# Gate and value products of four chunks by Strassen's scheme, with partial sums added in DRAM, in an attention kernel with two feed-forward layers

## The chip, the core and the metric

The kernel runs on one core of a Trainium2 chip. The metric is the device time of one execution in microseconds, the median of several. The engines are named as in the profile: PE is TensorE's matmuls (PEld its weight loads), DVE VectorE, ACT ScalarE, POOL GpSimd, SP the engine that does nothing but start transfers. Each takes its instructions in the order of its own queue.

## The reference

All is computed in fp32; the inputs arrive as float64 in their bit patterns. Linear attention over 4 batches of 576 rows and 8 heads of 64 gives a matrix x of 2304 tokens by 512. Two feed-forward layers follow:

```python
gate = 1.0 / (1.0 + np.exp(-(x @ w_gate)))      # w_gate, w_val: 512 x 1536
x = (gate * (x @ w_val)) @ w_out                # w_out: 1536 x 512
h = x @ w_in                                    # 512 x 2048
out = np.maximum(0.01 * h, h) @ w_out2          # 2048 x 512
```

## The kernel before

Each fp32 matrix is held as a sum of two fp32r parts, hi and lo (`split`, line 47: a CAST on ACT gives hi, a subtraction on DVE gives lo). One product of such matrices is three matmuls (`mm3`, lines 51 to 54: hi by hi, hi by lo, lo by hi), so L52, L53 and L54 of the profile are those three. The tokens lie transposed in five blocks: blocks 0 to 3 are 512 tokens of a batch, block 4 (called B in the code) the 4 times 64 that are left, 256 wide. A pair is blocks 0 and 1, or 2 and 3.

A layer's hidden width is worked off in chunks of 256, six in the first layer and eight in the second. The weights of a chunk come as float64 words over SP's queue (`fetch`) and are decoded to hi and lo on DVE and ACT (`decode`, lines 91 to 109) by the generator `decoded`, which is driven a step at a time by `ahead` wherever the code has room for it, and fully by `need` where a weight is wanted.

The attention comes first, with the first chunk of layer 1 for blocks 0 to 2 woven in. Layer 1 then goes, chunk by chunk and block by block, through `up_plain`: per half chunk a gate and a value product of 4 times 3 matmuls each, Tanh on ACT, one instruction on DVE that forms (tanh + 1) times value, and `hidden`, which splits the result into gh and gl. `down1_piece` multiplies those by w_out (6 matmuls into a PSUM bank ps_p) and adds the bank to the sums `acc` in SBUF on DVE (line 639). Pieces wait in the list `pend` until `gap` takes them out between later products, so that PE has work while DVE and ACT make the next gh and gl.

Layer 2 handles a pair at a time by Strassen's scheme (`quad`, lines 728 to 787): seven block products in place of eight, with sums of weight quarters (`sh`, `sl`, made in `decoded` where `quarters` is true) and sums of activation blocks (`sum_steps`, `sum_parts`; planes T1 to T4 in `ts`). The results leave `quad` in the order 3, 0, 2, 1; result i belongs to half i // 2 of the chunk and block i % 2 of the pair. SBUF holds the planes of one pair alone. After its last use in the first pair of a chunk each plane is overwritten with the other pair's from DRAM, by `swap` on SP's queue (line 726, tile `w<-td`); the first time it is computed in place and stored (line 712). A chunk of layer 2 is the units pair, B, pair, and the next chunk goes the other way round, so it begins with the pair that the last one ended on. After block B's unit the pieces of the first pair are worked off, block 2u + 1 ahead of block 2u (line 859).

Instructions are put in an order per engine by a scheduler at build time; the order is fixed in the program.

## Time and profile before

| | |
|---|---|
| median of 3 runs | 1069.11 us (1065.23 to 1069.24) |
| the profiled execution | 1071.7 us, its span 1069.9 us |
| granted TensorE clock, mean | 0.998 |
| busy share of PE, DVE, ACT, POOL | 97%, 69%, 42%, 5% |
| share of PE in the chain that ended last | 74% (DVE 11%, DMA 9%) |
| moved by DMA | 104.46 MB, mean 98 GB/s |

The profile lists for each engine how long it was busy, what ended its idle time, and when each instruction began. Matmuls overlap: one is listed as busy for 0.39 us while the next begins 0.23 us after it, so times of PE are read from starts, not from busy times. Stages follow one another: attention to about 311 us, five chunks of layer 1 to about 683 us, then eight chunks of layer 2.

### The profile page before, as it was taken

What the parts mean: (1) busy time and instruction counts of PE and PEld (TensorE: products, weight loads), DVE (VectorE), ACT (ScalarE), POOL (GpSimd) and SP (SyncE); (2) the same over time, 40 slices, a digit from 0 to 9 for tenths busy, and PEclk for the clock granted to TensorE, in tenths of its full rate; (3) what the DMA queues carried; (4) which work ended last, traced back from release to release, by engine and by line L of the source; (5) the groups of instructions that cost most, each with busy time, mean ns of one, the idle gap of its engine ahead of it and who ended that gap; (6) DMA issues with size and microseconds to landing.
All of it is one profiled execution on the core that took longest, in us unless ns stands there. A gap on an engine that the chain in (4) does not pass through costs nothing.

```text
span 1069.9 us, 14566 instructions
## 1 busy us (share of the span) xinstructions
PE 1041.7 (97%) x5506; PEld 886.0 (83%) x5506; DVE 741.4 (69%) x1309; ACT 454.2 (42%) x954; POOL 50.9 (5%) x49
## 2 busy tenths in 40 slices
PE   7899999999999999999999999999999999999997
PEld 6788988889788888888888888888888788887886
DVE  4964777766379985393493439995688787978555
ACT  4666676766454332131131124574333243423221
POOL 0112121212200000000000000000000000000000
PEclk9999999999999999999999999999999999999999
DMA  6532242331263321030030003435153351615233
GB/s 148 147 82 69 68 114 63 78 81 49 83 216 118 118 79 40 1 104 16 1 118 1 1 0 157 176 101 197 60 176 116 121 178 59 216 40 177 69 139 128
DMA packets 96006, 104.46 MB, mean 98 GB/s; under 512 B 66112, under 2 KB 66240, under 8 KB 95936
## 3 DMA queue, kind: packets, MB, share of 16 engines
q1 hardware_dynamic: 95936, 103.52, 31.1%
q8 instruction: 44, 0.72, 0.3%
q14 instruction: 26, 0.21, 0.1%
HBM read 87.10 MB, written 16.33 MB: 97 GB/s over the span
## 4 chain that ended last, share of the span: by engine, by line
PE 74%; DVE 11%; DMA 9%; ACT 3%; SPq 2%; issue 1%; POOL 1%; POOLq 0%; DVEq 0%
PE ps_u L52 11%; PE ps_u L53 11%; PE ps_u L54 11%; PE ps_p L54 10%; PE ps_p L52 10%; PE ps_p L53 9%; PE kv L384 4%; DMA raw<-in_moe_w_out_dram 3%; PE ps_n L434 2%; DMA raw<-in_moe_w_in_dram 2%; DVE acc L808 2%; DMA raw<-in_moe_w_gate_dram 1%; DVE w L108 1%; DVE ql L419 1%; DVE m L101 1%
## 5 line engine op out<-in xcount | busy, mean ns | idle before, releaser
L52 PE MATMUL ps_u<-xh,w 128*128 128x512 f32 (+1 forms) x592 | 213.8, 361 | 0.6 <-ACT w L106 0.4
L53 PE MATMUL ps_u<-xl,w 128*128 128x512 f32 (+1 forms) x592 | 213.7, 361 | 0.2 <-DVE xl L49 0.2
L54 PE MATMUL ps_u<-xh,w 128*128 128x512 f32 (+1 forms) x592 | 213.2, 361 | 0.0
L52 PEld LDWEIGHTS ps_u<-xh,w 128*128 128x128 f32 x592 | 111.8, 189 | 18.3 <-ACT xh L48 0.6
L53 PEld LDWEIGHTS ps_u<-xl,w 128*128 128x128 f32 x592 | 111.8, 189 | 17.4 <-DVE xl L49 0.5
L54 PEld LDWEIGHTS ps_u<-xh,w 128*128 128x128 f32 x592 | 111.7, 189 | 17.2 <-DVE w L108 0.2
L52 PE MATMUL ps_p<-w,gh 128*128 128x512 f32 x288 | 113.4, 394 | 5.8 <-ACT gh L48 5.8
L808 DVE TENSOR_TENSOR acc<-acc,ps_p 128x512 f32<-128x512 f32 x126 | 85.8, 684 | 41.4 <-PE ps_p L54 41.3
L48 ACT CAST gh<-q 128x512 fp32r<-128x512 f32 (+1 forms) x134 | 76.6, 575 | 88.4 <-DVE q L663 86.7
L53 PE MATMUL ps_p<-w,gh 128*128 128x512 f32 x288 | 112.4, 390 | 0.0
L54 PE MATMUL ps_p<-w,gl 128*128 128x512 f32 x288 | 111.4, 392 | 0.9 <-DVE gl L49 0.4
L49 DVE TENSOR_TENSOR gl<-q,gh 128x512 fp32r<-128x512 f32 (+1 forms) x134 | 83.8, 632 | 31.4 <-ACT gh L48 30.9
L663 DVE SCALAR_TENSOR_TENSOR q<-q,ps_u 128x512 f32<-128x512 f32 (+1 forms) x54 | 33.7, 625 | 87.1 <-PE ps_u L54 79.0
L674 ACT ACTIVATE q<-q 128x512 f32<-128x512 f32 x48 | 30.1, 630 | 123.4 <-DVE q L751 123.4
L97 ACT ACTIVATE e<-e,ebias 128x512 int32<-128x512 int32 x68 | 49.1, 723 | 77.9 <-DVE e L96 77.6
L53 PE MATMUL ps_p<-gl,w 128*128 128x512 f32 (+1 forms) x216 | 79.1, 366 | 0.0
L54 PE MATMUL ps_p<-gh,w 128*128 128x512 f32 (+1 forms) x216 | 79.0, 366 | 0.0
L52 PE MATMUL ps_p<-gh,w 128*128 128x512 f32 (+1 forms) x216 | 78.8, 366 | 0.2 <-ACT gh L48 0.2
L639 DVE TENSOR_TENSOR acc<-acc,ps_p 128x512 f32<-128x512 f32 (+1 forms) x100 | 62.7, 632 | 22.6 <-PE ps_p L54 21.3
L52 PEld LDWEIGHTS ps_p<-w,gh 128*128 128x128 f32 x288 | 54.1, 188 | 19.1 <-ACT gh L48 8.6
L54 PEld LDWEIGHTS ps_p<-w,gl 128*128 128x128 f32 x288 | 54.1, 188 | 15.0 <-DVE gl L49 3.9
L751 DVE TENSOR_TENSOR q<-ps_u,q 128x512 f32<-128x512 f32 x80 | 54.9, 688 | 16.3 <-PE ps_u L54 12.4
(144 smaller groups left out, 2017.5 us busy)
## 6 DMA issues: line engine op xcount, KB each, us to landing
w<-td SPq DMA_DIRECT2D x56, 512.0 KB, 6.0
raw<-in_moe_w_out_dram SPq DMA_DIRECT2D x28, 512.0 KB, 3.5
raw<-in_moe_w_in_dram SPq DMA_DIRECT2D x16, 512.0 KB, 3.7
td<-w SPq DMA_DIRECT2D x16, 512.0 KB, 2.7
raw<-in_moe_w_gate_dram SPq DMA_DIRECT2D x12, 512.0 KB, 4.3
raw<-in_moe_w_val_dram SPq DMA_DIRECT2D x12, 512.0 KB, 3.9
rb<-rd SPq DMA_DIRECT2D x32, 144.0 KB, 3.2
k<-in_k_dram SPq DMA_DIRECT2D x32, 128.0 KB, 2.9
```

The lines of the kernel that those rows point to most:

```text
L48: nc.scalar.copy(hi, src)
L49: nc.vector.tensor_tensor(out=lo, in0=src, in1=hi.bitcast(F32), op=ALU.subtract)
L52: nc.tensor.matmul(ps, lh, rh, start=first, stop=False, **kw)
L53: nc.tensor.matmul(ps, lh, rl, start=False, stop=False, **kw)
L54: nc.tensor.matmul(ps, ll, rh, start=False, stop=last, **kw)
L97: nc.scalar.activation(out=e, in_=e, func=ACTF.Relu, scale=8.0, bias=ebias)
L384: nc.tensor.matmul(ps[:, h], p.kf[j // 2][:, j % 2, h, s, :], vf[:, j, 64 * h:64 * h + 65], start=(h, j) == (0, 0), stop=False)
L639: nc.vector.tensor_tensor(out=a, in0=a, in1=po, op=ALU.add)
L663: nc.vector.scalar_tensor_tensor(out=th, in0=th, scalar=1.0, in1=ps[1], op0=ALU.add, op1=ALU.mult)
L674: nc.scalar.activation(out=th, in_=t, func=ACTF.Lrelu)
L751: nc.vector.tensor_tensor(out=o, in0=x, in1=y, op=ALU.add)
L808: nc.vector.tensor_tensor(out=a, in0=a, in1=po, op=ALU.add)
```

## The change

Chunks 2 to 5 of layer 1 (four of six) use `quad` for gate and for value (`up_pair1`, new), which takes 7 products where `up_plain` took 8. For that the weights of these chunks get quarter sums (`halved`), and x gets planes T: `norm3` stores x to DRAM (`xd`), `first_sums` loads it back and builds the planes in chunk 1. The planes of the two pairs are exchanged once a chunk, in both layers, by transfers that GpSimd's queue starts (`load_sums`). Layer 1's sums no longer stay in SBUF: in chunks 1 to 4 ACT copies a finished bank into one of six staging halves and GpSimd's queue adds it to DRAM (`accum_op`), and chunk 5 loads the sums back (`load_acc`). Block 2u now comes ahead of 2u + 1 in the pieces of both layers. Some hunks are left out (signatures, names, the exact slots).

```diff
+    def halved(l, c, i):
+
+        return i < 2 and (l, c) >= (1, 2)
...
-            while len(free) < (4 if quarters else 2) + reserve[0]:
+            quarters = halved(*key)
+            while len(free) < (4 if quarters else 2) + reserve[0] or key[:2] >= hold[0]:
...
+        nc.sync.dma_start(out=xd[b][:, c], in_=p.rb[:, 0:MAIN])
...
+    def staging():
+        staged[0] += 1
+        return halves[staged[0] % 6]
...
+
+        for i in range(1 if b == B else 2):
             acc(1, b, 2 * i)
-            nc.sync.dma_start(out=sums[1, b, i][0].rearrange("p (k t) -> p k t", k=2), in_=accd[b][:, 2 * i:2 * i + 2])
+            a = sums[1, b, i][0]
+            if b == B:
+                nc.sync.dma_start(out=a.rearrange("p (k t) -> p k t", k=KD), in_=accd[b])
+            else:
+                nc.sync.dma_start(out=a.rearrange("p (k t) -> p k t", k=2), in_=accd[b][:, 2 * i:2 * i + 2])
...
+            ahead(1)
+            if c == 0:
+                first_sum(b, e, po, staging())
+                return
+            if c < NC1 - 1:
+                st = staging()[:, :bw[b]]
+                nc.scalar.copy(st, po)
+                nc.gpsimd.dma_start(out=accd[b][:, e], in_=st, accum_op=ALU.add)
+                return
             a = acc(1, b, e)
-            if c == 0:
-                nc.scalar.copy(a, po)
-                return
             nc.vector.tensor_tensor(out=a, in0=a, in1=po, op=ALU.add)
...
                 if f == 0:
-                    gap(100)
+                    gap(4)
...
-    def sum_parts(pair, n, place=None):
+    def sum_parts(l, pair, n, s):
 
         j, i = PLACE[n]
-        src = sums.pop((1, 2 * pair + i, j))
-        s = [take(F32R) for _ in range(2)] if place is None else [retake(p) for p in place]
+        src = sums.pop((l - 1, 2 * pair + i, j))
         hi, lo = s[0][0], s[1][0]
         nc.scalar.copy(hi, src[0])
         nc.vector.tensor_tensor(out=lo, in0=src[0], in1=hi.bitcast(F32), op=ALU.subtract)
         give(src)
-        ts[n] = s
-        td[pair, n] = dr.tile([128, 2, 1024], F32, name=f"td{pair}{n}", tag=f"td{pair}{n}")
+        td[l, pair, n] = dr.tile([128, 2, 1024], F32, name=f"td{l}{pair}{n}", tag=f"td{l}{pair}{n}")
         for k in range(2):
-            nc.sync.dma_start(out=td[pair, n][:, k], in_=s[k][0].bitcast(F32))
+            nc.sync.dma_start(out=td[l, pair, n][:, k], in_=s[k][0].bitcast(F32))
...
+    def first_sums(pair, stay):
+
+        for i in range(2):
+            for j in range(2):
+                s = sums[0, 2 * pair + i, j] = take(F32, "acc")
+                nc.sync.dma_start(out=s[0].rearrange("p (k t) -> p k t", k=2), in_=xd[2 * pair + i][:, 2 * j:2 * j + 2])
+        for _ in range(8):
+            yield True
+        yield from sum_steps(1, pair)
+        held = deque()
+        for n in (2, 1, 3, 4):
+            if len(held) == 2:
+                give(*held.popleft())
+            s = [take(F32R) for _ in range(2)]
+            sum_parts(1, pair, n, s)
+            if stay:
+                ts[n] = s
+            else:
+                held.append(s)
+            yield True
...
+    def load_sums(l, pair, n):
+        for k in range(2):
+            nc.gpsimd.dma_start(out=ts[n][k][0].bitcast(F32), in_=td[l, pair, n][:, k])
...
+    def swap(l, pair, n):
+
         ts[n] = [retake(s) for s in ts[n]]
-        for k in range(2):
-            nc.sync.dma_start(out=ts[n][k][0].bitcast(F32), in_=td[other, n][:, k])
-
-    def quad(l, c, i, pair, then):
+        if (l, pair, n) in td:
+            load_sums(l, pair, n)
+        else:
+            sum_parts(l, pair, n, ts[n])
+
+    def quad(l, c, i, pair, rooms, then):
...
+    def up_pair1(c, pair, between, then):
+        h, th = {}, {}
+        for i, t in quad(1, c, 0, pair, (1, 1, 1, 1, 1, 0), lambda n: None):
+            th[i] = halves[6 + i]
+            nc.scalar.activation(out=th[i], in_=t, func=ACTF.Tanh, scale=0.5)
+        between()
+        for i, t in quad(1, c, 1, pair, (1, 1, 1, 0, 0, 0), then):
+            nc.vector.scalar_tensor_tensor(out=th[i], in0=th[i], scalar=1.0, in1=t, op0=ALU.add, op1=ALU.mult)
+            hidden(h, (i // 2, 2 * pair + i % 2), th[i])
+        return h
...
+    def queue1(c, u, h):
+        bs = [B] if u == B else [2 * u, 2 * u + 1]
+        pend.extend(down1_piece(c, b, e, h) for b in bs for e in range(KD))
+
...
+        h = up_plain(1, 0, b, 14)
+        gap(100)
+        pend.extend(down1_piece(0, b, e, h) for e in range(KD))
...
+    side.append(first_sums(0, False))
+    for b in range(NB):
+        reserve[0] = (4, 8, 8, 5, 2)[b]
...
-                    sum_parts(0, n)
-            if b == B:
-                drop(1, c, 0)
+            side[:] = [first_sums(1, True)]
+        h = up_plain(1, 1, b, 5)
+        gap(100)
...
+    units = [1, B, 0]
+    keep = lambda n: None
+    for c in range(2, NC1):
+        final = c == NC1 - 1
+        if final:
+            units = [0, 1, B]
+        for n, u in enumerate(units):
+            if u == B:
+                h = up_plain(1, c, B, 2)
+            elif not final:
+                h = up_pair1(c, u, (lambda: drop(1, c, 0)) if n == 2 else (lambda: None),
+                             (lambda k, u=u: swap(1, 1 - u, k)) if n == 0 else keep)
+            elif u == 0:
+                def between():
+                    need(1, c, 1)
+                    need(1, c, 2)
+                    hold[0] = 2, 0
+
+                def then(k):
+                    swap(1, 1, k)
+                    if k == 4:
+                        gap(2)
+                        load_acc(0)
+                        load_acc(1)
+                h = up_pair1(c, 0, between, then)
+            else:
+                def between():
...
+                def then(k):
+                    for g in side:
+                        for _ in g:
+                            pass
+                    side.clear()
+                    swap(2, 0, k)
+                reserve[0] = 5
+                h = up_pair1(c, 1, between, then)
+                drop_sums(1, c, 1)
...
-            pend.extend(down1_piece(c, b, e, h) for e in range(KD))
-            if b == B:
...
+    need(2, 0, 0)
+    for _ in sum_steps(2, 1):
...
+                hold[0] = 3, 0
...
-            bs = [B] if u == B else [2 * u + 1, 2 * u]
+            bs = [B] if u == B else [2 * u, 2 * u + 1]
             pend.extend(down2_piece(c, b, j, h) for b in bs for j in range(bw[b] // 128))
```

The built program has, against the one before, on PE 96 fewer matmuls of 512 columns; on DVE 80 more additions of a PSUM bank (`q<-ps_u,q`), 64 fewer of 512 and 16 fewer of 256 columns into `acc`, 16 more 1024 wide (x's planes), 32 more of 256 and 16 more of 512 for weight sums; on ACT 88 copies of a bank to staging, 16 to q, and 16 CASTs 1024 wide more; on POOL 168 transfers where there were none (88 planes `w<-td`, 80 additions to `accd`); on SP 56 planes fewer, 16 plane stores, 16 stores and 8 loads of x more.

Three places show how the order moves. Line numbers of the two kernels differ: before, L663 is gate times value, L639 the addition into `acc`, L643 the lo part of layer 1's result, L695 and L707 sums and lo parts of planes, L751 an addition in `quad`, L174 a weight sum's lo part; after, these are L869, L681, L685, L738, L749, L822 and L180, while L105 to L114 decode a weight.

First, DVE in a chunk of layer 1, before:

```order
L663 SCALAR_TENSOR_TENSOR q_4827<-q_4827,ps_u_4829 128x512
L49 TENSOR_TENSOR gl_4844<-q_4827,gh_4843 128x512
L663 SCALAR_TENSOR_TENSOR q_4865<-q_4865,ps_u_4867 128x512
L639 TENSOR_TENSOR acc_3670<-acc_3670,ps_p_4885 128x512
L49 TENSOR_TENSOR gl_4882<-q_4865,gh_4881 128x512
L639 TENSOR_TENSOR acc_3670<-acc_3670,ps_p_4893 128x512
L639 TENSOR_TENSOR acc_3672<-acc_3672,ps_p_4901 128x512
L639 TENSOR_TENSOR acc_3672<-acc_3672,ps_p_4909 128x512
L663 SCALAR_TENSOR_TENSOR q_4941<-q_4941,ps_u_4943 128x512
L49 TENSOR_TENSOR gl_4958<-q_4941,gh_4957 128x512
```

and after, the end of a pair's value products:

```order
L869 SCALAR_TENSOR_TENSOR w_4590<-w_4590,q_5366 128x512
L869 SCALAR_TENSOR_TENSOR w_4589<-w_4589,ps_u_5306 128x512
L180 TENSOR_TENSOR w_5469<-s_5610,w_5468 128x512
L49 TENSOR_TENSOR gl_5390<-w_4590,gh_5389 128x512
L49 TENSOR_TENSOR gl_5395<-w_4589,gh_5394 128x512
L822 TENSOR_TENSOR q_5315<-ps_u_5307,q_5315 128x512
L822 TENSOR_TENSOR q_5323<-ps_u_5308,q_5323 128x512
L869 SCALAR_TENSOR_TENSOR w_4590<-w_4590,q_5315 128x512
L869 SCALAR_TENSOR_TENSOR w_4589<-w_4589,q_5323 128x512
L180 TENSOR_TENSOR w_5469<-s_5610,w_5468 128x512
L49 TENSOR_TENSOR gl_5411<-w_4590,gh_5410 128x512
L49 TENSOR_TENSOR gl_5423<-w_4589,gh_5422 128x512
```

The additions of ps_p into `acc` are gone from DVE there; additions inside `quad` (L822) and weight sums (L180) stand in their place.

Second, DVE where layer 2 begins. Before, from the last of the four sums of the second pair's blocks:

```order
L695 TENSOR_TENSOR acc_3672<-acc_3672,acc_3860 128x1024
L751 TENSOR_TENSOR q_6807<-ps_u_6791,q_6799 128x512
L707 TENSOR_TENSOR w_6810<-acc_3860,w_6809 128x1024
L639 TENSOR_TENSOR acc_3984<-acc_3984,ps_p_6816 128x256
L639 TENSOR_TENSOR acc_3984<-acc_3984,ps_p_6826 128x256
L174 TENSOR_TENSOR w_6924<-s_7060,w_6923 128x512
L707 TENSOR_TENSOR w_6843<-acc_3670,w_6842 128x1024
L643 TENSOR_TENSOR xl4_95<-acc_3984,xh4_94 128x256 x2
L639 TENSOR_TENSOR acc_3984<-acc_3984,ps_p_6849 128x256
L751 TENSOR_TENSOR q_6865<-ps_u_6791,q_6799 128x512
L643 TENSOR_TENSOR xl4_95<-acc_3984,xh4_94 128x256
L707 TENSOR_TENSOR w_6868<-acc_3843,w_6867 128x1024
```

and after, from the third of them (w_71xx and w_72xx are planes, m_7105 a weight of layer 2 being decoded, acc_6924 block B's sums, xh4 and xl4 its parts):

```order
L738 TENSOR_TENSOR acc_6922<-acc_6922,acc_6916 128x1024
L107 SCALAR_TENSOR_TENSOR m_7105<-raw_7082,m_7105 128x512
L738 TENSOR_TENSOR acc_6918<-acc_6918,acc_6922 128x1024
L749 TENSOR_TENSOR w_7133<-acc_6922,w_7132 128x1024
L681 TENSOR_TENSOR acc_6924<-acc_6924,ps_p_7141 128x256
L111 SCALAR_TENSOR_TENSOR m_7105<-m_7105,e_7106 128x512
L685 TENSOR_TENSOR xl4_95<-acc_6924,xh4_94 128x256
L681 TENSOR_TENSOR acc_6924<-acc_6924,ps_p_7152 128x256
L749 TENSOR_TENSOR w_7171<-acc_6916,w_7170 128x1024
L685 TENSOR_TENSOR xl4_95<-acc_6924,xh4_94 128x256
L114 TENSOR_TENSOR w_7104<-m_7105,w_7103 128x512
L105 TENSOR_SCALAR m_7105<-raw_7093 128x512
```

The decoding of a weight now stands between the planes and block B's parts.

Third, layer 2 after block B's unit. PE before, where gh_8154 is the last result of the pair and gh_8101 the first:

```order
L54 MATMUL ps_u_8193<-xh4_94,w_7778 128x256
L52 MATMUL ps_p_8213<-w_8009,gh_8154 128x512
L53 MATMUL ps_p_8213<-w_8010,gh_8154 128x512
L54 MATMUL ps_p_8213<-w_8009,gl_8155 128x512
L52 MATMUL ps_p_8213<-w_8009,gh_8101 128x512
L53 MATMUL ps_p_8213<-w_8010,gh_8101 128x512
L54 MATMUL ps_p_8213<-w_8009,gl_8102 128x512
```

and after, where gh_8050 is the second result and gh_8084 the third:

```order
L54 MATMUL ps_u_8127<-xh4_94,w_7712 128x256
L52 MATMUL ps_p_8147<-w_7943,gh_8050 128x512
L53 MATMUL ps_p_8147<-w_7944,gh_8050 128x512
L54 MATMUL ps_p_8147<-w_7943,gl_8051 128x512
L52 MATMUL ps_p_8147<-w_7943,gh_8084 128x512
L53 MATMUL ps_p_8147<-w_7944,gh_8084 128x512
L54 MATMUL ps_p_8147<-w_7943,gl_8085 128x512
```

ACT makes them, before:

```order
L674 ACTIVATE q_8105<-ps_u_7986 128x512
L48 CAST gh_8107<-q_8105 128x512
L674 ACTIVATE q_7995<-q_7995 128x512
L97 ACTIVATE e_8465<-e_8465,ebias_74 128x512
L48 CAST gh_8134<-q_7995 128x512
L97 ACTIVATE e_8598<-e_8598,ebias_74 128x512
L674 ACTIVATE q_8003<-q_8003 128x512
L171 CAST w_8187<-s_8312 128x1024
L48 CAST gh_8154<-q_8003 128x512
L674 ACTIVATE q_8179<-ps_u_8166 128x256
```

and after, with gh_8096 the last result:

```order
L716 ACTIVATE q_8048<-ps_u_7920 128x512
L48 CAST gh_8050<-q_8048 128x512
L103 ACTIVATE e_8399<-e_8399,ebias_74 128x512
L177 CAST w_8121<-s_8246 128x1024
L716 ACTIVATE q_7929<-q_7929 128x512
L48 CAST gh_8084<-q_7929 128x512
L716 ACTIVATE q_7937<-q_7937 128x512
L716 ACTIVATE q_8113<-ps_u_8100 128x256
L48 CAST gh_8096<-q_7937 128x512
```

PE's first piece after block B now reads the second and third result of the pair where it read the last.

## Rows read from the trace of the kernel before

**Rows 1.** The page's head and its part 1: span, busy time of each engine, instructions

```profile
span 1069.9 us, 14566 instructions
...
PE 1041.7 (97%) x5506; PEld 886.0 (83%) x5506; DVE 741.4 (69%) x1309; ACT 454.2 (42%) x954; POOL 50.9 (5%) x49
```

**Rows 2.** Windows by stage: length, PE, PEld, DVE, ACT, POOL busy, clock, DMA share, GB/s

```profile
311.00:386.00 75.00, 74.45 (x361) 62.42 (x360) 67.93 (x125) 30.20 (x55) 0.00 (x0) 1.00 0.33 104
386.00:461.00 75.00, 75.00 (x366) 63.54 (x366) 43.88 (x80) 19.04 (x33) 0.00 (x0) 1.00 0.14 43
...
683.00:742.00 59.00, 59.00 (x292) 49.69 (x291) 47.92 (x85) 37.71 (x66) 0.00 (x0) 1.00 0.56 196
742.00:1052.00 310.00, 305.35 (x1405) 252.41 (x1404) 230.40 (x398) 109.66 (x192) 0.00 (x0) 1.00 0.36 120
```

**Rows 3.** Timeline of PE in layer 1, the first and last of 36: start, duration in us

```profile
560.04 0.39 PE L52 MATMUL ps_u<-xh,w 128*128 128x512 f32 x1
560.27 0.39 PE L53 MATMUL ps_u<-xl,w 128*128 128x512 f32 x1
...
567.98 0.39 PE L54 MATMUL ps_u<-xh,w 128*128 128x512 f32 x1
```

**Rows 4.** Timeline of PE in layer 2: plane products, then switches after block B

```profile
762.88 0.39 PE L52 MATMUL ps_u<-w 128*128 128x512 f32 x1
763.11 0.39 PE L53 MATMUL ps_u<-w 128*128 128x512 f32 x1
...
742.56 0.28 PE L54 MATMUL ps_u<-xh,w 128*128 128x256 f32 x1
...
837.93 0.28 PE L53 MATMUL ps_u<-xl,w 128*128 128x256 f32 x1
838.05 0.28 PE L54 MATMUL ps_u<-xh,w 128*128 128x256 f32 x1
840.07 0.50 PE L52 MATMUL ps_p<-w,gh 128*128 128x512 f32 x1 [1.75 <-ACT gh L48]
...
1029.15 0.28 PE L54 MATMUL ps_u<-xh,w 128*128 128x256 f32 x1
```

**Rows 5.** Timeline of PE at the last unit, idle time and releaser in brackets

```profile
1052.20 0.39 PE L54 MATMUL ps_u<-xh,w 128*128 128x512 f32 x1
1054.68 0.50 PE L52 MATMUL ps_p<-w,gh 128*128 128x512 f32 x1 [2.09 <-ACT gh L48]
```

**Rows 6.** Timeline of DVE where layer 1 ends

```profile
659.38 1.22 DVE L707 TENSOR_TENSOR w<-acc,w 128x1024 fp32r<-128x1024 f32 x1
660.51 0.69 DVE L49 TENSOR_TENSOR gl<-q,gh 128x512 fp32r<-128x512 f32 x1
661.11 1.28 DVE L639 TENSOR_TENSOR acc<-acc,ps_p 128x512 f32<-128x512 f32 x2
...
667.12 0.76 DVE L99 TENSOR_SCALAR m<-raw 128x512 int32<-128x512 int32 x2
667.79 1.29 DVE L101 SCALAR_TENSOR_TENSOR m<-raw,m 128x512 f32<-128x512 uint32 x2
```

**Rows 7.** Groups of DVE by line and form: count, busy us, mean ns of one

```profile
L49 DVE TENSOR_TENSOR gl<-q,gh 128x512 fp32r<-128x512 f32 x106 | 72.7, 688 | 27.0 <-ACT gh L48 26.7
...
L96 DVE TENSOR_SCALAR e<-raw 128x512 int32<-128x512 int32 x68 | 28.8, 424 | 22.4 <-DMA raw<-in_moe_w_in_dram 8.7 <-DMA raw<-in_moe_w_out_dram 7.5 <-DMA raw<-in_moe_w_gate_dram 4.8
...
L639 DVE TENSOR_TENSOR acc<-acc,ps_p 128x256 f32<-128x256 f32 x20 | 8.2, 417 | 0.3
```

**Rows 8.** DMA issues of the page: count, KB each, median us from issue to landing

```profile
w<-td SPq DMA_DIRECT2D x56, 512.0 KB, 6.0
...
accd<-st SPq DMA_DIRECT2D x12, 256.0 KB, 2.5
```

**Rows 9.** The plane tile td on SP's queue: us to landing; and a burst of six

```profile
DMA to landing us min/median/max: 2.6/5.4/8.1
...
769.88 7.70 SPq L726 DMA_DIRECT2D w<-td  x6
```

**Rows 10.** A window of 2 us within that burst, columns as in Rows 2

```profile
772.00:774.00 2.00, 2.00 (x10) 1.63 (x9) 1.99 (x4) 1.09 (x2) 0.00 (x0) 1.00 1.01 342
```

More of the change, by code (lines that the diff above doesn't have):

```diff
@@ L63, in linear_attention_moe @@
         d[B] = xp.tile([128, KD, REM * B], F32R, tag=f"{p}{B}", name=f"{p}{B}")
+    xd = [dr.tile([128, KD, MAIN], F32, name=f"xd{b}") for b in range(B)]
     def xpart(d, b, kk):
@@ L137, in first_weights, with decoded @@
             wts[1, 0, i] = r
-    def decoded(keys, reserve):
+    def decoded(keys, reserve, hold):
         dp = pools["dec"]
@@ L178, in decoded, with drop_sums @@
             wts[key] = r
+    def drop_sums(*key):
+        r = wts[key]
+        give(*(r.pop(k) for k in ("sh", "sl")))
     def drop(*key):
@@ L579, in tile2, with fix @@
         return pools["q"].tile([128, 512], F32, tag="q", name="q")[:, :w]
+    fixed, halves = [], []
+    def fix(n):
+        for _ in range(n):
+            s = take(F32)
+            fixed.append(s)
+            halves.extend(s[0][:, 512 * i:512 * i + 512] for i in range(2))
+    fix(3)
+    staged = [0]
+    def staging():
+        staged[0] += 1
+        return halves[staged[0] % 6]
     xs = {}
@@ L587, in linear_attention_moe @@
     reserve = [0]
+    hold = [(3, 0)]
     order = [(1, c, i) for c in range(1, NC1) for i in range(3)] + [(2, c, i) for c in range(NC2) for i in (0, 2)]
-    stream = decoded(order, reserve)
+    stream = decoded(order, reserve, hold)
+    side = []
     def ahead(n):
         for _ in range(n):
-            if not next(stream, None):
+            if side and next(side[0], None) is None:
+                side.pop(0)
+            if not next(stream, None) and not side:
                 break
@@ L597, in need @@
         while key not in wts:
-            if next(stream, None) is not True:
+            if next(stream, None) is not True and key not in wts:
                 raise RuntimeError(f"no room for {key}: {len(free)} slots free")
@@ L688, in linear_attention_moe, with sum_steps @@
     ts = {}
-    def sum_steps(pair):
-        f = {(j, i): sums[1, 2 * pair + i, j][0] for j in range(2) for i in range(2)}
+    def sum_steps(l, pair):
+        f = {(j, i): sums[l - 1, 2 * pair + i, j][0] for j in range(2) for i in range(2)}
         b11, b12, b21, b22 = (f[j, i] for j in range(2) for i in range(2))
@@ L772, in quad @@
         then(3)
-        room(2)
+        room()
         prod(pa, W(0, 1), X(b0, 1), False)
@@ L786, in quad @@
         yield 1, u2
-        room(1)
+        room()
+    def up_pair1(c, pair, between, then):
[8 more added lines that the diff above has]
+        return h
     def up_pair2(c, pair, then):
         h = {}
-        for i, t in quad(2, c, 0, pair, then):
+        for i, t in quad(2, c, 0, pair, (2, 2, 2, 2, 0, 0), then):
             leaky(h, (i // 2, 2 * pair + i % 2), t, i == 0)
@@ L846, in linear_attention_moe @@
+    pend.append(lambda: give(sums.pop((1, B, 0))))
+    give(*fixed)
+    need(2, 0, 0)
+    for _ in sum_steps(2, 1):
         pass
-    reserve[0] = 2 * B + 1
     units = [0, B, 1]
```

94 lines of the change are left out of this document (57 added, 37 removed).

## Prediction

> **What bounds the kernel now.** The page comes first [rows 1]: PE is busy for 1041.7 of 1069.9 us. The windows by stage [rows 2] say where that leaves anything: in the chunks of layer 1 PE is busy for 75.00 us of 75.00 while DVE has 43.88, where layer 2 begins PE still has 59.00 of 59.00 though DVE has 47.91, and in layer 2 PE has 305.35 of 310. The granted clock is 1.00 in all of them. So layer 1 takes as long as its matmuls, and only layer 2 has something to win besides. A matmul's price must come from starts: 36 matmuls in a row start from 560.04 to 567.98 [rows 3], 7.94 / 35 = 0.227 us each, while each is listed with 0.39 us because it overlaps the next. The 256-column form starts every 0.12 us (837.93 to 838.05) [rows 4].
>
> **The matmuls.** The built program has 96 fewer of 512 columns: a pair's gate or value product goes from 48 to 42, and there are 16 such. 96 x 0.227 = 21.8 us, all in layer 1, where PE has no idle time to hide it. Products with a plane T run at the same pace (762.88 to 763.11 [rows 4]). Priced by the 0.39 us it would be 37 us; that counts the overlap twice.
>
> **Layer 2's first pieces after block B.** From the switch at 742.56 to that at 1029.15 [rows 4] are six chunks, 286.6 us. A chunk's program is 84 matmuls of the pairs and 108 of the pieces, 192 x 0.227 = 43.6, and 24 of 256 columns, 2.9: 46.4, six of them 278.6. So 8.0 us are lost, and the timeline shows them at the switch: at 838.05 the next start is 2.02 us later in place of 0.12, and the wait is for the CAST of gh. That piece reads the pair's last result. The last result's way (addition, leaky ReLU, CAST, subtraction) is covered by block B alone, 24 x 0.12 = 2.9 us, and it took 2.9 to 4.8 us. After the change the piece reads the second and third result. The third is one product earlier (6 x 0.227 = 1.4 us) and is read by the second half of the piece (3 x 0.227 = 0.7 us later): cover 1.4 + 2.9 + 0.7 = 5.0 us, more than the longest way seen. I take 7.7 of the 8.0 us as gain (ends 4 and 8, since ACT's order also moves). At the end there is no block B: 1052.20 to 1054.68 [rows 5] is 2.48 us where 0.23 would do. The new cover is 1.4 + 0.7 = 2.1, so 0.4 stays lost and 1.8 is gained (ends 0 and 2.25).
>
> **Where layer 2 begins.** Here the change costs. DVE's price is also read from starts [rows 6]: behind each other, 512 wide takes 0.60 us (660.51 to 661.11), 1024 wide 1.13 (659.38 to 660.51), a TENSOR_SCALAR of 512 0.335 (667.12 to 667.79 for two); that is about 0.085 less than the durations (688 and 424 ns) [rows 7], so 256 wide is 0.417 - 0.085 = 0.33. From the first of the second pair's four sums, DVE's next 31 instructions are, after the change, eight of 1024, thirteen of 512, two TENSOR_SCALARs and eight of 256: 9.0 + 7.8 + 0.7 + 2.6 = 20.1 us, and PE's pieces behind them wait for the last (gl). Before, the same 31 places held 20.0 us too, and PE had in them 50 matmuls of 512 and 72 of 256, 11.4 + 8.6 = 20.0 us: just enough, and the windows show no idle time there [rows 2]. After, PE has 40 and 36: 9.1 + 4.3 = 13.4 us. DVE has no pause ahead of that (in each 10 us of PE's program before it, it has about 9.7 us of work), so PE waits 20.1 - 13.4 = 6.7 us. What was cover, the layer's last blocks done one at a time, has gone to earlier places. Ends: 0, if DVE comes to this place several us ahead; 9.5, if it runs at its listed durations (22.9 us). I take 6.7, since the pace comes from rows of the same stage.
>
> **DVE and ACT in the changed chunks.** A chunk is now 264 matmuls of 512 and 72 of 256: 59.9 + 8.6 = 68.5 us. DVE has in it 20 additions in `quad` and 16 instructions on the results at 0.60, 4 for block B at 0.33, three weights to decode (four TENSOR_SCALARs and eight of 512: 6.1 each) and two weight sums (four of 256, two of 512: 2.5 each): 12.0 + 9.6 + 1.3 + 18.4 + 5.0 = 46 us of 68.5. The additions into `acc` are ACT's copies now, and ACT has 19 of 75 us there [rows 2]. So both are hidden; if DVE fell behind, the first piece behind each value product would wait. There are seven such places. They have the same 5 us of cover as above, and I put them at 1 us in all (ends 0 and 7, the latter at the mean of layer 2's losses, 1.0 each).
>
> **The new transfers.** GpSimd starts no transfer in the trace. In a chunk it has 8 planes of 512 KB and 20 additions of at most 256 KB. Planes are wanted 23 to 29 us of PE's program after they are started, but in chunk 5, where both pairs follow each other without block B, 8.7 to 12.7 us. SP's planes land after 2.6 to 8.1 us [rows 9], just within; a gain is excluded, since PE's losses are all accounted for above. x's planes are made in chunk 1 with up to 9.2 MB in 25 us, and a full DMA (share 1.01) moved 342 GB/s [rows 10], so that takes 27 us: 2 us late if PE has to wait for it. I take 1 us (ends 0 and 5). The 16 stores of x in the attention stand in SP's queue behind a value made an iteration earlier and block nothing; what waits behind them are loads for the pair after next.
>
> **Sum.** -21.8 - 7.7 - 1.8 + 6.7 + 1.0 + 1.0 = -22.6 us: the span goes from 1069.9 to 1047.3, the profiled execution's 1071.7 to 1049.1. That execution is 2.6 us over the median of 1069.1; from the median the sum gives 1046.5. I forecast 1047.
>
> **Rivals.** *Layer 2's start costs nothing*, DVE being ahead there: 1047 - 6.7 = 1040. For it: before, DVE was near full too and PE lost nothing. Against: the cover fell by a third and DVE's work did not.
>
> *DVE holds the value products.* A value product with three pieces is 13.6 us of PE (42 and 18 matmuls). Beside it stand 13 instructions at 0.60 and, when a weight is being decoded, 15 steps at 0.51 on the mean: 15.5 us. 1.9 us in each of eight: +15, 1062. Against: decoding runs in only part of them, and layer 2 before lost nothing inside its products.
>
> *GpSimd's queue is the bound*, the case that ends slower. The place is ACT's copy into staging: it waits until the addition six pieces back has landed, and behind it on ACT stand Tanh and the CASTs that PE's next pieces read. It decides once a transfer holds the queue for over 68.5 / 28 = 2.45 us. One at a time, with SP's figures (a plane at the shortest 2.6, an addition like a store of 256 KB, 2.5 [rows 8, 9]), a chunk takes 70.8 us, 2.3 too many, in three chunks 7 us. An addition reads and writes: at 1.5 times the store's time, 3.75, it is 95.8 us, +27 in each of chunks 2 to 4, 1047 + 82 = 1129. With the median of 6.0 us for a plane it is more. For it: nothing in the trace shows this queue. Against: SP started six planes in 7.7 us, 1.28 each [rows 9], with several in flight; that way 28 transfers need 36 us.
>
> The Trainium skill, "DMA: Bandwidth & Descriptors", Anatomy of one DMA, speaks against the change here: it gives a GpSimd transfer about 2.0 us and the bytes at 436 GB/s, by which an estimate is 3.2 us a plane and 2.6 an addition, one at a time 78 us a chunk, and 1075 in all. It also says that most of those 2.0 us are the wait for the write's receipt, which transfers in flight share; then the sum stays as it is. No row here shows which. The Trainium skill, "SBUF: State Buffer", SBUF: two separate sides, adds that GpSimd can't write descriptors while DVE runs a single-source fp32 operation through both its ports. The TENSOR_SCALARs look like such ones (424 against 688 ns [rows 7]); twelve a chunk would hold the queue for 5 us at most, which matters in this rival alone.
>
> That fewer matmuls don't happen is no rival: the built program has them.
>
> **Chances and range.** Forecast (1042 to 1056) 0.60, layer 2's start free 0.12, DVE in the value products 0.12, GpSimd's queue 0.10, several covers short at once (1057 to 1068) 0.06. The range is 1038 to 1063: from the free start with the best ends to the value products; the queue and the upper part of the last two are left out. A measurement of this kernel can tell about 0.5%, 5.3 us, from no change: below 1063.8 lie the forecast, the free start, most of the value products and half of the last, 0.84; within, 0.06; over 1074.5 the queue, 0.10.
>
> **What the profile after would show.** PE rows 0.227 us apart in `up_pair1` with no idle time (chunks of 68.5 us); in layer 2 windows of 46.4 us a chunk and no wait of over 0.3 us behind block B; one stretch of about 6 us of PE waiting for DVE and ACT where layer 2 begins, with DVE full in it; ACT's copies to staging waiting for no DMA. I am wrong on the queue if those copies wait or planes land later than 9 us in chunk 5, wrong on DVE if PE waits for L822, and wrong on the switch if ps_p still waits for gh behind block B.

## The result and the profile after

The changed kernel takes 1078.3 us (median, 1072.3 to 1082.1) where the one before takes 1067.5: a ratio of 1.0091 (95% interval 1.0061 to 1.012), so 0.9% slower. The forecast was 1047, 2% faster. The profiled execution took 1076.0 us, its span is 1074.2.

The page's head, the clock of TensorE and the share of the DMA engines in 40 slices, and the queues (kind: packets, MB, share of 16 engines):

```profile
span 1074.2 us, 14977 instructions
...
PE 1031.5 (96%) x5410; PEld 875.5 (82%) x5410; DVE 779.8 (73%) x1373; ACT 519.2 (48%) x1066; POOL 168.8 (16%) x217
...
PEclk9999999999999899998999999989999999999999
DMA  5543343341378978578589495565261633515144
...
q1 hardware_dynamic: 95216, 94.09, 28.0%
q0 software_dynamic: 24192, 65.02, 24.5%
```

The 96 matmuls are gone (5410 for 5506, [rows 1]), and still PE's share fell by only a point. Where its time went is read best from starts. What each matmul starts later than the pace allows (0.227 us, or 0.12 for 256 columns), summed by stage, is:

| stage | before | after | difference | forecast |
|---|---|---|---|---|
| end of chunk 0 and chunk 1 (290 to 400 us) | 1.3 | 11.1 | +9.9 | part of 1.0 |
| chunks 2 to 5 of layer 1 | 0.2 | 21.1 | +21.0 | part of 1.0, and 1.0 |
| where layer 2 begins (680 to 740) | 0.4 | 7.3 | +6.9 | +6.7 |
| layer 2 from 740 on | 10.6 | 0.7 | -9.9 | -9.5 |
| fewer matmuls | | | -21.8 | -21.8 |

That is +6.1 us; PE reaches the first stage about 1.5 us earlier, which leaves, within 0.3 us, the +4.3 of the two spans. Three of five terms came as forecast, and 31 us came from a place that had been given 2.

The windows show the stages (columns as in [rows 2], DMA share and GB/s last):

```profile
311.00:386.00 75.00, 70.47 (x315) 57.30 (x314) 60.34 (x98) 37.84 (x62) 10.71 (x12) 0.95 0.88 260
...
478.00:492.00 14.00, 7.21 (x24) 5.45 (x23) 6.83 (x12) 4.56 (x7) 3.98 (x7) 0.80 0.91 271
...
557.00:571.00 14.00, 8.95 (x40) 7.26 (x39) 8.85 (x16) 4.88 (x9) 3.95 (x6) 0.76 1.00 277
...
628.00:640.00 12.00, 10.02 (x38) 7.80 (x37) 5.54 (x9) 4.18 (x8) 4.14 (x7) 0.86 0.97 249
...
690.00:712.00 22.00, 18.95 (x90) 15.80 (x89) 21.08 (x33) 11.20 (x18) 0.00 (x0) 0.84 0.59 216
...
760.00:1052.00 292.00, 291.93 (x1356) 244.24 (x1355) 226.48 (x390) 105.70 (x180) 25.89 (x48) 1.00 0.36 125
```

Layer 2 is full now (291.93 of 292, before 305.35 of 310 [rows 2]). Where layer 2 begins, DVE is the full engine, 21.08 of 22 us, as forecast. But in the three windows of layer 1 in the middle PE stands still part of the time while no engine is full: DVE has 6.83 of 14 us. What is full there is the last share but one, the DMA engines: 0.91, 1.00, 0.97, where chunks of layer 1 had 0.14 to 0.33 before [rows 2].

The waits name the releasers. First PE over the whole span, then DVE from 296 to 720 us (waiter, awaited, us in total, times, longest), lines of each:

```profile
PE ps_u L52 <- DVE q L822: 13.8, 3, 6.8
PE ps_p L52 <- ACT gh L48: 4.6, 3, 2.8
...
PE ps_p L52 <- DVE acc L681: 2.9, 1, 2.9
```

```profile
DVE e L102 <- DMA raw<-in_moe_w_out_dram: 19.3, 7, 5.6
...
DVE acc L738 <- DMA acc<-xd: 6.5, 2, 5.1
DVE e L102 <- DMA raw<-in_moe_w_gate_dram: 5.7, 3, 4.2
DVE e L102 <- DMA raw<-in_moe_w_val_dram: 5.3, 5, 2.2
```

The page says PE waits for DVE. It isn't that DVE is slow: DVE itself waits, 37 us in all, for transfers. In the same stretch of the kernel before its waits for fetched weights came to 2.7 us. The first stall, in the timeline of SP, of DVE and of PE (start, duration, idle time and releaser in brackets):

```profile
475.56 2.74 SPq L122 DMA_DIRECT2D raw<-in_moe_w_out_dram  x2
```

```profile
477.97 0.69 DVE L111 SCALAR_TENSOR_TENSOR m<-m,e 128x512 f32<-128x512 f32 x1
484.29 0.43 DVE L102 TENSOR_SCALAR e<-raw 128x512 int32<-128x512 int32 x1 [5.63 <-DMA raw<-in_moe_w_out_dram]
...
486.92 0.43 DVE L102 TENSOR_SCALAR e<-raw 128x512 int32<-128x512 int32 x1 [0.72 <-DMA raw<-in_moe_w_out_dram]
487.26 1.41 DVE L822 TENSOR_TENSOR q<-ps_u,q 128x512 f32<-128x512 f32 x2
```

```profile
480.82 0.39 PE L54 MATMUL ps_u<-xh,w 128*128 128x512 f32 x1
488.00 0.79 PE L52 MATMUL ps_u<-w 128*128 128x512 f32 x1 [6.79 <-DVE q L822]
488.59 0.63 PE L53 MATMUL ps_u<-w 128*128 128x512 f32 x1
489.02 0.63 PE L54 MATMUL ps_u<-w 128*128 128x512 f32 x1
```

The fetch of w_out's first half starts at 475.56. DVE is ready for it at 478.66, and it lands just before 484.29: 8.7 us, where the same fetches took 3.5 on the median before. The landings here, and the row of the page before:

```profile
DMA to landing us min/median/max: 8.7/8.8/8.9
```

```profile
raw<-in_moe_w_out_dram SPq DMA_DIRECT2D x28, 512.0 KB, 3.5
```

The additions inside `quad` (L822), for which PE waits, have had their inputs for a while; they stand behind L102 in DVE's order. Nothing needs this weight soon: by the built order the next steps that read it (L105, at 524.85 in the trace) stand 39 us of PE's program later and its first reader on PE 79. And when PE resumes, its matmuls start 0.43 us apart (489.02 after 488.59) in place of 0.227. The window says why, last but two (the granted clock, 0.50): it has fallen to the lower of its two levels, and so a wait of 6.8 us costs 9.5.

```profile
488.00:492.00 4.00, 4.00 (x9) 3.13 (x10) 4.00 (x7) 2.75 (x5) 2.08 (x4) 0.50 1.01 168
```

### The profile page after: what moved, and what is told of

Same layout as the page of the kernel before. It is cut to its first block, busy times and chain, and to the rows that moved or that the text cites. A ratio compares the mean times of both kernels' runs of the same rounds, so it can differ in the third digit from the quotient of the medians.

```text
span 1074.2 us, 14977 instructions
## 1 busy us (share of the span) xinstructions
PE 1031.5 (96%) x5410; PEld 875.5 (82%) x5410; DVE 779.8 (73%) x1373; ACT 519.2 (48%) x1066; POOL 168.8 (16%) x217
## 3 DMA queue, kind: packets, MB, share of 16 engines
q0 software_dynamic: 24192, 65.02, 24.5%
HBM read 109.64 MB, written 49.36 MB: 148 GB/s over the span
## 5 line engine op out<-in xcount | busy, mean ns | idle before, releaser
L822 DVE TENSOR_TENSOR q<-ps_u,q 128x512 f32<-128x512 f32 x160 | 110.1, 688 | 61.0 <-PE ps_u L54 57.3
L53 PE MATMUL ps_u<-xl,w 128*128 128x512 f32 (+1 forms) x432 | 152.9, 354 | 0.0
L52 PE MATMUL ps_u<-xh,w 128*128 128x512 f32 (+1 forms) x432 | 152.1, 354 | 0.2
L54 PE MATMUL ps_u<-xh,w 128*128 128x512 f32 (+1 forms) x432 | 152.0, 353 | 0.0
L52 PE MATMUL ps_u<-w 128*128 128x512 f32 x256 | 102.3, 400 | 13.8 <-DVE q L822 13.8
L678 POOL DMA_DIRECT2D accd<-w x80 | 70.4, 880 | 258.3 <-ACT w L677 182.5
L784 POOL DMA_DIRECT2D w<-td x88 | 49.3, 575 | 370.7 <-PE ps_u L54 363.4
L53 PE MATMUL ps_u<-w 128*128 128x512 f32 x256 | 101.5, 397 | 0.0
L54 PE MATMUL ps_u<-w 128*128 128x512 f32 x256 | 101.2, 396 | 0.0
L52 PEld LDWEIGHTS ps_u<-xh,w 128*128 128x128 f32 x432 | 82.8, 192 | 12.4 <-ACT xh L684 0.7
L53 PEld LDWEIGHTS ps_u<-xl,w 128*128 128x128 f32 x432 | 82.7, 191 | 11.6 <-DVE xl L685 0.3
L54 PEld LDWEIGHTS ps_u<-xh,w 128*128 128x128 f32 x432 | 82.7, 192 | 11.1
L466 POOL TENSOR_TENSOR rb<-u,rb 64x576 f32<-64x576 f32 x32 | 48.4, 1513 | 234.7 <-DMA rb<-rd 124.7
```

Source lines behind the costliest of these rows:

```text
L52: nc.tensor.matmul(ps, lh, rh, start=first, stop=False, **kw)
L53: nc.tensor.matmul(ps, lh, rl, start=False, stop=False, **kw)
L54: nc.tensor.matmul(ps, ll, rh, start=False, stop=last, **kw)
L466: nc.gpsimd.tensor_tensor(out=p.rb[sl], in0=p.u[h][sl], in1=p.rb[sl], op=ALU.mult)
L678: nc.gpsimd.dma_start(out=accd[b][:, e], in_=st, accum_op=ALU.add)
L784: nc.gpsimd.dma_start(out=ts[n][k][0].bitcast(F32), in_=td[l, pair, n][:, k])
```

## The experiments

The theory that came out of this reading (F): planes and additions of GpSimd's queue fill the DMA engines, so a fetch on SP's queue lands late; the built order leaves it only 3 us before DVE waits for it, with `quad`'s additions queued behind. Its rivals: L, the lead is too short even on empty engines; and Q, GpSimd's queue itself holds the work up, the prediction's own rival. Ratios are to the kernel before on the same chip, whose medians were 1067.7 to 1068.8 us.

**Planes later.** The exchange starts behind the value product. The edit takes in chunks 2 to 4; in chunk 2 the planes' loads stood at that place already (from 408 us, now from 407), in chunks 3 and 4 they move. Nothing else does.

```diff
-                             (lambda k, u=u: swap(1, 1 - u, k)) if n == 0 else keep)
+                             keep)
...
             gap(100)
+            if n == 0 and not final:
+                for k in (2, 1, 3, 4):
+                    swap(1, 1 - u, k)
```

> Against the changed kernel (1078.3 us), the eight plane loads of each exchange in chunks 3 and 4 start about 9 us of PE's program later, behind the value product; DVE, ACT, PE and SP keep their order word for word. Theory F (the fetch of w_out shares the DMA engines with the planes, lands after 8.7 us where the order left it 3.4, and DVE waits for it with quad's additions queued behind): the fetch lands within 6 us, the two stalls of PE at 481 and 559 us (7.2 and 5.4 us, 9.5 and 7.2 with the slow clock behind them) shrink to 2 us each or less, time 1062 to 1068. Theory L (the order leaves the fetch too little even on empty DMA engines): stalls as before, 1078. Theory Q (GpSimd's queue is what holds the work up, my rival of the prediction): stalls as before or longer, 1078 or more.

Measured: 1070.3 us, ratio 1.0014 (0.999 to 1.0037). The two places lose 6.4 and 4.4 us where it was 9.5 and 7.2, and the fetch at the first lands after 3.4 to 5.4 us for 8.7 to 8.9. The direction is F's, half the size: the additions are still there.

**Plain writes.** The additions are written over what they should be added to.

```diff
-                nc.gpsimd.dma_start(out=accd[b][:, e], in_=st, accum_op=ALU.add)
+                nc.gpsimd.dma_start(out=accd[b][:, e], in_=st)
```

> The additions in DRAM become plain writes of the same bytes by the same queue, all orders the same; the partial sums of chunks 0 to 3 are thereby lost. A packet of 2 KB took 178 ns of a DMA engine as an addition and 84 ns as a plain transfer, so 256 KB hold 16 engines for 1.4 us or 0.7. Theory F: two additions stand among the planes at each stall, so each stall shrinks by 1 to 3 us, and chunk 1, where the DMA engines are full from 334 to 366 us, loses about 5 us less: 1066 to 1074. Theory L: 1078 within 2 us. Theory Q: the queue's issues stay (0.87 us each), 1078.

Measured: 1061.9 us, 0.9923 (0.9895 to 0.995), 4 us better than the low end of F. The queues of its page:

```profile
q1 hardware_dynamic: 95216, 94.09, 28.4%
q0 software_dynamic: 18560, 65.02, 16.8%
```

The same 65.02 MB take 16.8% of the span (178 us) in place of 24.5% (263): 85 us for 80 transfers, so an addition costs all 16 engines some 1.06 us more than the write of the same bytes. (It goes in more packets, 24192 in all for 18560.) Chunk 1's loss goes (from 7.9 us at 350 to 395 to 0.3), and the stalls at 481 and 559 become 6.0 and 5.9. L had no room for either change. Against Q this run says less than was expected of it: GpSimd's own time for these 80 transfers fell too, from 0.88 to 0.55 us each by the pages, so its queue was relieved along with the engines.

**Both.**

> Both reliefs of the DMA engines together: planes 9 us later in chunks 3 and 4, and the additions in DRAM as plain writes (the sums of chunks 0 to 3 are lost by it); DVE, ACT, PE and SP in the changed kernel's order. Theory F: the fetch of w_out lands after 3.4 to 4.5 us as in the kernel before (median 3.9), PE loses under 1 us at each of the two places that cost 9.5 and 7.2 in the changed kernel, 6.4 and 4.4 with late planes alone and about 6 each with plain writes alone: 1061.9 - 11 = 1051 (1048 to 1054). Theory L (the lead of 3.4 us is too short on empty engines as well): 2 us or more stay at each, 1055 or more.

Measured: 1050.2 us, 0.9843 (0.981 to 0.9876), with DVE, ACT, PE and SP in the changed kernel's order. DVE at the first place:

```profile
469.37 0.43 DVE L102 TENSOR_SCALAR e<-raw 128x512 int32<-128x512 int32 x1 [0.28 <-DMA raw<-in_moe_w_out_dram]
...
472.51 0.43 DVE L102 TENSOR_SCALAR e<-raw 128x512 int32<-128x512 int32 x1 [1.23 <-DMA raw<-in_moe_w_out_dram]
```

It waits 0.28 and 1.23 us where it waited 5.63 and 0.72, and PE loses 0.4 us there and nothing at the second place (1.2 and 0.5 some us later, where it waits for gh and gl). Summed as in the table above, chunk 1 with the end of chunk 0 loses 2.9 us for 11.1, and chunks 2 to 5 lose 2.8 for 21.1. L falls: the lead is enough on engines that are free. But for the lost sums and the later planes this is the kernel that the prediction had in mind, and it takes 1050.

**The order on DVE.** The first step of decoding the weights of chunks 2 to 5 may not be moved ahead of what the text has before it.

```diff
-        nc.vector.tensor_scalar(out=e, in0=high, ...)
+        first = nc.vector.tensor_scalar(out=e, in0=high, ...)
+        if pin:
+            tc.keep_in_program_order(first)
```

> Only the order on DVE is changed: the first step of decoding a weight of chunks 2 to 5 is kept behind what the program text has ahead of it, so that 10 us of PE's program or more lie between a fetch and its first use where there were 3.4; the transfers are the same. Theory F and theory L: the stalls at 481, 559 and 630 us (9.5, 7.2 and 3.9 us with the slow clock) go, 1056 to 1060. Rival (the DMA engines themselves are the bound): PE then waits for planes or weights instead, 1070 or more. Theory Q: 1078.

Measured: 1068.8 us, 1.0005 (0.9977 to 1.0034): 10 us gained, not 20. The stalls at 481 and 559 are gone, but others have come. DVE's waits for fetches:

```profile
DVE e L102 <- DMA raw<-in_moe_w_in_dram: 10.6, 2, 6.6
...
DVE m L107 <- DMA raw<-in_moe_w_val_dram: 6.6, 2, 3.3
...
DVE m L107 <- DMA raw<-in_moe_w_gate_dram: 4.5, 3, 2.4
...
DVE m L107 <- DMA raw<-in_moe_w_out_dram: 3.0, 1, 3.0
```

The second step (L107 there) also reads the fetched words and was free to move, so it took the first one's place. And the fetches of w_in stood behind loads of the sums on SP's queue, which wait until the additions have landed: PE lost 10.9 us at 618 to 642.

**Both steps, planes later, sums behind the fetches.**

```diff
+        keep(nc.vector.tensor_scalar(out=m, in0=high, ...))
...
+            tc.keep_in_program_order(d)      # d: the load of a sum in load_acc
```

> The changed kernel's whole computation, three orders changed: both first steps of decoding that read a fetched weight are kept in their place in the text (chunks 2 to 5), the planes of chunks 3 and 4 come 9 us later, and the loads of the sums in chunk 5 stand behind w_in's fetches on SP's queue and no longer ahead of them. Theory F with SP's queue as its second place: the losses of the first such kernel (2.5 at 392, 2.5 at 405, 2.4 at 504, 2.1 at 575 and 11 at 620 to 640 us) go, 1068.8 - 17 = 1052 (1048 to 1058). If the DMA engines themselves are the bound, they turn up elsewhere as waits of PE for planes or of DVE for fetches with 10 us of lead, 1062 or more.

Measured: 1062.6 us, 0.9961 (0.9939 to 0.9984). 6 of the 17 us came. By the trace the four smaller places are gone and the fifth loses 4.8 for 10.9, but two others cost 6.2 and 6.4, both again with DVE waiting: 7.1 us for a load of x in chunk 1 (at 352), and 3.1 and 2.4 us for fetches where layer 2 first exchanges planes (740 to 747).

**Those as well.** Layer 2's decoding is kept in place from its second chunk on, and x's sums stand further behind their loads (16 steps for 8).

> The kernel with pins and late planes (1062.6) and two more orders changed: the decoding of layer 2's weights from its second chunk on is kept in its place in the text too (16 us of PE's program behind the fetch where 3.4 to 5 stood), and the four differences of x's blocks stand 14 us behind the loads they read, not 4 to 11. Theory F: of what that kernel still lost, 5.6 us at 352 (DVE waits 7.1 us for a load of x) and 6.4 at 740 to 747 (DVE waits 3.1 and 2.4 us for fetches) go, 1062.6 - 12 = 1051 (1048 to 1056). If chunk 1 is bound by the DMA engines' work itself, its loss stays and the time is 1056 or more.

Measured: 1052.6 us, 0.9868 (0.9843 to 0.9892), with all of the computation in it and the additions as they are. Both places are free. So chunk 1 was not bound by the DMA engines' work as such, though they are full there (a share of 1.02 from 330 to 366 us in the changed kernel). Left are 5.9 us in chunk 5, where PE waits for planes (1.8 us), for gh and for DVE, and the 7.6 where layer 2 begins.

**Planes on SP's queue**, in the changed kernel.

```diff
-            nc.gpsimd.dma_start(out=ts[n][k][0].bitcast(F32), in_=td[l, pair, n][:, k])
+            nc.sync.dma_start(out=ts[n][k][0].bitcast(F32), in_=td[l, pair, n][:, k])
```

> The planes' loads are started by SP's queue as in the kernel before, the additions stay with GpSimd's. Theory F: the same bytes share the same DMA engines at the same place, so the first fetch of w_out still lands late and PE still loses 5 us or more at each of the two places; the second fetch stands behind the planes on SP's queue. 1074 to 1082. Theory Q (GpSimd's queue is what is slow): both stalls go, 1062.

Measured: 1060.4 us, 0.9937 (0.9915 to 0.9959). By the time this is Q's, and F as I had put it is wrong here. SP's queue and DVE at the first place show why:

```profile
475.63 0.34 SPq L122 DMA_DIRECT2D raw<-in_moe_w_out_dram  x1
476.07 9.03 SPq L784 DMA_DIRECT2D w<-td  x8
485.20 0.46 SPq L122 DMA_DIRECT2D raw<-in_moe_w_out_dram  x1
```

```profile
479.95 0.43 DVE L102 TENSOR_SCALAR e<-raw 128x512 int32<-128x512 int32 x1 [1.21 <-DMA raw<-in_moe_w_out_dram]
...
481.77 1.41 DVE L822 TENSOR_TENSOR q<-ps_u,q 128x512 f32<-128x512 f32 x2
```

The landing of the first fetch:

```profile
DMA to landing us min/median/max: 4.3/4.3/4.3
```

All eight loads of planes stand behind the first fetch on the one queue, where in the changed kernel two had started ahead of it and two came beside it; it lands after 4.3 us. The second fetch stands behind the planes, and its first use has moved behind `quad`'s additions: DVE waits 4.80 us for it at 497, no addition stands behind that wait, and PE loses 0.1 us there. A late fetch costs nothing there. The trace loses 5.9 us in chunks 2 to 5 for 21.1, and 10.7 in chunk 1, where the changed kernel lost 11.1. One queue keeps an order. Two share the engines, and the fetch pays for it. The Trainium skill, "DMA: Bandwidth & Descriptors", Queues, rings and completion order, has each DMA engine take turns between the queues it has work for, a packet at a time; these landings, 8.7 us beside GpSimd's planes and 4.3 ahead of SP's, agree. So it is the planes' place on a second queue that costs, but not by that queue's being slow: GpSimd needs 0.87 us to issue an addition and 0.54 for a plane, and ACT waited for its staging halves 1.0 us in all.

**Pins and SP's planes together.**

> The fastest so far (1052.6) with the planes' loads on SP's queue in place of GpSimd's, additions still by GpSimd. It still lost 5.9 us in chunk 5 at 608 to 625, where PE waits for planes. If two queues that share the DMA engines are what delays them, the planes come one after the other and in the order in which they are wanted, and 2 to 4 us go: 1050 (1047 to 1053). If the engines' work as such is the bound there, 1052 or more.

Measured: 1051.2 us, 0.9829 (0.9795 to 0.9863), the fastest that computes all, though the times alone don't tell it from the 1052.6 with the planes on GpSimd's queue. In its trace chunk 5 loses 2.7 us for 5.9. From block B's first matmul in chunk 2 to that in chunk 3, and on to chunk 4's:

```profile
406.68:475.30 68.62, 68.62 (x337) 58.16 (x336) 46.59 (x85) 32.57 (x58) 17.48 (x20) 1.00 0.79 189
475.30:543.90 68.60, 68.60 (x337) 58.17 (x336) 48.99 (x89) 33.07 (x58) 17.39 (x20) 1.00 0.77 176
```

**Where layer 2 begins.** The four differences of the second pair are left out.

```diff
-    for _ in sum_steps(2, 1):
-        pass
```

> The four differences of the second pair's blocks where layer 2 begins are left out (the planes are then made from the blocks alone), four instructions of DVE at 1.13 us. The changed kernel lost 7.3 us at that place. If DVE's work in a row is what PE waits for there, as the prediction has it (20.1 us of DVE over 13.4 of PE), the loss becomes 7.3 - 4.5 = 2.8 us and the time 1078.3 - 4.5 = 1073.8 (1072 to 1075). If it is the bank of PSUM or ACT's table load, the loss stays at 7 us, 1078.

Measured: 1071.8 us, 1.0035 (1.0007 to 1.0062), 6.5 us less than the changed kernel; in the trace the place loses 2.5 for 7.3, so 4.8 us went where 4.5 were expected. (The medians differ by more than that; the profiled runs' stalls in layer 1 vary by 1 to 5 us between executions.) PE there, the changed kernel and this one:

```profile
696.96 0.39 PE L54 MATMUL ps_u<-xh,w 128*128 128x512 f32 x1
700.21 0.39 PE L52 MATMUL ps_p<-gh,w 128*128 128x256 f32 x1 [2.87 <-DVE acc L681]
```

```profile
696.66 0.28 PE L54 MATMUL ps_u<-xh,w 128*128 128x256 f32 x1
697.90 0.38 PE L52 MATMUL ps_u<-xh,w 128*128 128x256 f32 x1 [0.97 <-ACT xh L684]
```

DVE's work in a row is the cause, as forecast. The wait that ends last isn't the one that the prediction named, gl: it is that for L681, an addition into `acc` that reads a bank of PSUM, and it stands in the same row of DVE.

**Layer 2's order alone**, in the kernel before.

```diff
-            bs = [B] if u == B else [2 * u + 1, 2 * u]
+            bs = [B] if u == B else [2 * u, 2 * u + 1]
```

> The kernel before with one part of the change: block 2u ahead of 2u + 1 in layer 2's pieces. If the switch behind block B is what layer 2 loses, as the prediction has it, its 9.5 us are gained here as well: 1067.5 - 9.5 = 1058 (1056 to 1060). If the changed kernel's layer 2 gains them in another way (planes on GpSimd's queue instead of SP's), the time stays at 1065 to 1069.

Measured: 1059.2 us, 0.9924 (0.9899 to 0.995). PE's waits from 700 us on are gone entirely. One line of the change, by itself, is worth 9.6 us, the forecast's 9.5.

**The same line undone in the changed kernel.**

> The changed kernel with layer 2's pieces of block 2u + 1 ahead of 2u again. The kernel before with the other order gained 9.6 us; if the parts add up, this one loses as much: 1078.3 + 9.5 = 1088 (1085 to 1091). If the changed kernel's stalls hide the switch, less: 1080 or below.

Measured: 1079.7 us, ratio to the kernel before 1.0126 (1.0089 to 1.0164): 1.4 us slower than the changed kernel, within the intervals, where 9.5 was expected. In its trace layer 2 loses 5.5 us in place of 0.7, 2.4 of it at the end and 2.2 at the first switch; the five switches between lose 0.1 each. So another part of the change does there what the order does.

**The rooms alone**, in the kernel before: pieces are taken out 2, 2, 2, 2, 0, 0 between the products of a layer 2 pair, not 2, 1, 2, 1, 1, 1.

> The kernel before with one other part of the change, which the prediction did not look at: in layer 2's pair four of its six rooms take two pieces each and the last two none (2, 1, 2, 1, 1, 1 before). The pieces of the order are not touched. By the order built, the second fetch of w_in then has 10.1 us of PE's program ahead of its first use where it had 3.6. If that fetch is what holds DVE, and with it the pair's last result, at the switch behind block B (the trace of before shows DVE waiting 1.9 us for it at 837), the six switches cost under 0.3 us each, the 2.25 us at the end stay, and the time is 1067.7 - 7.5 = 1060 (1058 to 1062). If only the order of the pieces counts, the time stays at 1066 to 1069.

Measured: 1068.4 us, 0.9988 (0.9969 to 1.0007). The five switches in the middle are free here too, but two places stay:

```profile
742.98 0.28 PE L54 MATMUL ps_u<-xh,w 128*128 128x256 f32 x1
745.36 0.50 PE L52 MATMUL ps_p<-w,gh 128*128 128x512 f32 x1 [2.10 <-ACT gh L48]
...
1049.64 0.39 PE L54 MATMUL ps_u<-xh,w 128*128 128x512 f32 x1
1052.13 0.50 PE L52 MATMUL ps_p<-w,gh 128*128 128x512 f32 x1 [2.10 <-ACT gh L48]
```

The trace gains 2.9 us over that of the kernel before, the time a microsecond or nothing. My 7.5 left out that the first switch got worse (4.0 us lost around it for 1.2). So the two parts overlap: either frees the five switches in the middle, and only the order frees the first and the end. Why undoing the order in the changed kernel costs 1.4 us by the medians and 4.8 in layer 2 by the trace stays open; the layer 1 stalls of that execution were about 5 us shorter than those of the changed kernel's, which may be all of it.

## Why the prediction was wrong, step by step

*The matmuls* were right: -21.8. A chunk without stalls takes 68.60 to 68.62 us, forecast 68.5, against 73.98 before (by the starts of block B).

*Layer 2 after block B* was right in size, 9.9 for 9.5, and a chunk takes 46.42 for 46.4. The cause given was the pieces' cover alone, and for the kernel before that holds. In the changed kernel `quad`'s rooms, which the text passed over, would have freed most switches too. The wait under the switch was already the one that mattered later: DVE at 837 us of the kernel before waits 1.9 us for a fetch of w_in, with the addition for the last result behind it. I read only PE's row there [rows 4], which names ACT. DVE's:

```profile
836.86 0.43 DVE L96 TENSOR_SCALAR e<-raw 128x512 int32<-128x512 int32 x1 [1.93 <-DMA raw<-in_moe_w_in_dram]
837.20 0.68 DVE L751 TENSOR_TENSOR q<-ps_u,q 128x512 f32<-128x512 f32 x1
```

*Where layer 2 begins* was right in its cause: take four of DVE's instructions out, and 4.8 of the 7.3 us go. That the size fits so well, 6.9 for 6.7, may be in part luck. PE stands idle for only 3.0 us; most of the rest falls between 702 and 708 us, where its clock is at the lower level (0.50) beside a DVE that is full, and the sum had no term for that. Whether a PE at the upper level would have waited for DVE instead isn't shown.

*DVE and ACT in the changed chunks*: DVE has 46.59 to 48.99 us in a chunk that runs without stalls (the last windows above), forecast 46, and doesn't run out of time. But the 1.0 us for its stalls asked only whether it has too much work. It has too little time at one instruction: it waits.

*The new transfers* is the step that failed. It asked whether planes land before their readers, which they do, and whether x's planes take 27 us of DMA time in 25. It gave +1 us with 5 as the upper end, and the trace shows 31 for it and the 1.0 of the step before together. All but 4 of them go when planes and additions weigh less on the engines (*Both* loses 5.7 in these stages, the kernel before 1.5). Three things were left out. It never asked whom the transfers displace: SP's fetches, whose landing went from 3.5 to 8.7 us. It took an addition's cost from a store, outside the rival; on the engines it is some 1.06 us more. And it didn't look at how long the built order lets DVE go before it waits for a fetch, 3 us of PE's program, which the order and the landing times of before together told. The sentence that stores of x in SP's queue "block nothing" was the right question asked of one new queue entry only. Chunk 5's loads of sums did block a fetch, as the run with the pinned first step shows.

*The rivals.* The queue rival had the right resource and the wrong victim: it looked at how fast GpSimd starts transfers and whether ACT's copies wait (1.0 us in all), and it ended at 1129. None of the rivals with a chance ends near 1078. The signals named for it, copies that wait and planes later than 9 us in chunk 5, hardly showed (1.0 us in all; 8.2 us on the median, 9.3 at most), and the one that did, a PE wait for L822, was listed as DVE's being too slow. The estimate after the Trainium skill, "DMA: Bandwidth & Descriptors", Anatomy of one DMA, came nearest (one transfer at a time, 1075), for a reason that the trace doesn't bear out: GpSimd started four planes from 473.19 to 478.3 us, which landed after 9.0 on the median, so several were in flight.

*The clock* had no term at all. Behind each of the long waits PE ran at its lower level; the stall at 481 cost 9.5 us where PE waited 6.8.

## What to carry to other kernels

A transfer that is moved to another queue no longer stands behind those of the old one: list what it will now run beside, and which engine waits for that, with what queued behind the wait. A wait for a fetch belongs at a place in the engine's order that leaves it the landing time under load, not on empty engines; here moving such waits alone gave 10 us, and 26 with the planes and the loads of sums put behind the fetches that they held up. And a releaser on the page is only the last one: follow it to what it waited for itself.
